# Even and odd time steps in rising order, output rows in transfers of up to 128 partitions, the filter folded in SBUF, and a new order of steps

## The chip, the cores and the metric

The kernel runs on one core of one Trainium2 chip. The metric is the device time of one execution in microseconds: three runs of the kernel before gave 217.42, 217.69 and 217.69, median 217.69 us. All durations come from one further, profiled execution.

## What is computed

Linear attention without softmax, an RMS norm per head, and then a gated long convolution over time. The sizes are 8 batches, 8 heads, 576 time steps, 64 channels a head, so 512 channels.

```python
kv = np.einsum('bhsd,bhse->bhde', k, v)
out = np.einsum('bhsd,bhde->bhse', q, kv)
rms = np.sqrt(np.mean(out * out, axis=-1, keepdims=True) + 1e-06)
x = out / rms * g_norm                      # heads side by side: [8, 576, 512]
x1, x2, x3 = split(x @ w_proj)              # three times 512 channels
x2_conv = irfft(rfft(x2, axis=1) * rfft(filter_fft, axis=0))
y = x1 * x2_conv * x3
return y @ w_out                            # float32 [8, 576, 512]
```

## The kernel before, in words

Nothing is looped. A table, ORDER, lists 725 steps in the form name.batch, and each step records its instructions in that order. Every engine (TensorE, VectorE, ScalarE, GpSimd, SyncE) works through its own queue strictly in the order in which the steps were recorded, and waits there for what the next instruction needs. A third number after a step's name puts so many matmuls of zeros (line 113) ahead of it on TensorE. PSUM is four pairs of banks; a step takes the pair that was given back first, and waits until it is free.

For one batch the steps are these.

- Loads. GpSimd's DMA queue brings k and v (128 partitions) and q (96 partitions, each with six successive time steps) and casts them to bf16. K is 72 matmuls for the heads' kv; eK copies them to SBUF. T (12 transposes on TensorE) or Qt (a transposing DMA on SyncE's queue) turns q; GpSimd's one-element copy Qh waits for such a transposing DMA.
- O: eight matmuls of 288 columns give two heads at a time, channels on the partitions and time along the free axis. sq (line 471) squares them on ScalarE, ob or ov (lines 478, 476) copy them times g_norm, R sums the squares over a head by a matmul, rs takes the inverse root, and x (line 503, VectorE) is the product. x holds the normalised input of one batch, 128 partitions by four head pairs by 576 steps.
- The gates. Ga and Gb are the projections to x1 and x3, 32 matmuls of 288 columns for each 128 channels and each of the two (line 645). x1 is copied by ScalarE (line 651), and g (line 653, VectorE) multiplies the other with it.
- The convolution. eo (line 515) adds and subtracts x and x backwards in time; fa and fr fold the three thirds of the sequence; rrM, rrT, abM, abT project the folded pieces with the middle part of w_proj; err, eab, eT copy the results to SBUF. F0, F1, F1t, F2, F2c are the transform over time as matmuls with tables of sines; M0 and M1 (line 620, VectorE) multiply with the filter's transform, M2 (line 635) does the third part; A0 and A1 (line 626) add the two halves of the products, mostly on GpSimd, as Av sometimes on VectorE. Io and I are the way back; vB, w and fin (lines 685 to 697, VectorE) recombine and multiply with the gates into yg. The step fin can be cut in two halves of time and two of channels (f001, f101, f023, f123; w likewise).
- The output. U (line 730) multiplies 256 rows of yg with w_out, U4 (line 743) 128 rows shared by two batches, ot copies to SBUF as float32, and SyncE's queue sends it. For the last batch single blocks of 128 rows (V, line 768) are copied by va or vv (line 774) and sent from SyncE's and GpSimd's queues (line 779).

Along the free axis time lies in 18 blocks of 32 steps: thirds of the sequence, and in each the residues of six. So 32 successive columns are 32 rows of the output six rows apart, and every 128-row block of output is sent in four transfers of 32 partitions each.

Ahead of the first batch a preamble builds the tables. Angles are made on VectorE, sines on ScalarE, Tb (TensorE) transposes them, and copies put them in SBUF. The filter is loaded (Lf) and folded by 36 matmuls of 512 columns with pieces of the identity and of a reversed identity (Ff, line 326). H0, H1, H2 (lines 343, 346) transform it; ScalarE scales one half of each result (lines 354, 357) and VectorE adds the other (line 359). 21 matmuls of zeros stand ahead of the first transposes.

Of the kernel before, what the change touches and what calls it, by code (L numbers as in the profile page):

```python
# [19 lines left out]
ORDER = """Z.0 Zi.0 Zd.0 Zr.0 Lqa.0 Zt.0 An2.0 An01.0 T0.0.21 Lf.0 eTv0.0 Zf.0 Tb0.0.4 Tb1.0 Tb2.0 Lqb.0 Lva.0 Ff0.0 Ff2.0.2  # L20
Ff1.0 Act.0 T1.0 Lka.0 Ka.0 eKa.0 eTv1.0 H1.0 Lkb.0 O01.0 Lvb.0 Kb.0.6 sq0.0 R0.0 sq1.0 eKab.0 rs0.0 O23.0.1 ov1.0
Lq.1 sq2.0 ov0.0 R1.0 R2.0.3 ov2.0 T0.1 Lw1.0 sq3.0 rs1.0 x0.0 Lv.1 Lw3.0 R3.0 Lk.1 rs2.0 ov3.0 eo0.0 eTv0.1 rs3.0
fr0.0 x1.0 H2.0 H0.0 eo1.0 HN1.0 Ga2.0 Ga1.0 Gb2.0 x12.0 Lw2.0 Gb1.0 Lqa.3 x11.0 T1.1 g2.0 K.1 eTv1.1 Ga0.0 g1.0 eK.1
x10.0 Lvb.2 fr1.0 O01.1 sq1.1 rrM.0 rrT.0 fa.0 HN0.0 sq0.1 abM.0 err.0 ov0.1 ov1.1 F0.0 abT.0 eab.0 Lk.2 Lqb.3 eT.0
O23.1 F2c.0 Lva.2 M0.0 F2.0 sq3.1 Lq.2 ob3.1 sq2.1 Qt.3 Gb0.0 ob2.1 M2.0 F1t.0 F1.0 R0.1 A0.0 R2.1 g0.0 rs0.1 Ga3.0
rs2.1 x13.0 R1.1 M1.0 K.2 rs1.1 Qt.2 R3.1 rs3.1 eK.2 Av1.0 Qh.3 Gb3.0 Io01.0 x.1 Io23.0 eo.1 I23.0 oa01.0 ea23.0
oa23.0 fr.1 Ga0.1 I01.0.1 ea01.0 g3.0 Ga1.1 fa.1 Lka.3 rrM.1 rrT.1 x10.1 Lva.3 x11.1 vB.0 Lkb.3 err.1 O01.2 sq1.2
abT.1 abM.1 sq0.2 w.0 Lvb.3 eT.1 ob1.2 Gb0.1 eab.1 f001.0 ob0.2 F0.1 f101.0 f023.0 Lwo.0 O23.2 g0.1 sq2.2 Ga2.1 ob2.2
Lva.4 M0.1 sq3.2 Gb1.1 ob3.2 x12.1 F2c.1 f123.0 F2.1 R1.2 R0.2 g1.1 F1t.1 F1.1 rs1.2 Lqb.4 M2.1 R2.2 K.3 rs0.2 rs2.2
Gb2.1 R3.2 eK.3 rs3.2 M1.1 Ga3.1 Lqa.4 g2.1 Lk.4 x1.2 A0.1 O23.3 x13.1 Av1.1 Lq.5 Gb3.1 sq2.3 sq3.3 x0.2 ob3.3 g3.1  # L30
U0.0 ob2.3 Ga2.2 Io01.1 ot0.0 x12.2 oa01.1 I23.1 Io23.1 I01.1 eo.2 oa23.1 fa.2 fr.2 abT.2 ea01.1 Lvb.4 R2.3 Ga3.2 eT.2
rs2.3 ev23.1 O01.3 sq0.3 abM.2 x13.2 sq1.3 vB.1 w.1 ob1.3 rrM.2 eab.2 rrT.2 K.4 F1t.2 ov0.3 F1.2 Qt.5 R0.3 err.2 eK.4
rs0.3 Gb3.2 R1.3 rs1.3 fin.1 M1.2 Gb2.2 R3.3 g3.2 A1.2 F0.2 U4.1 Qt.4 Lqa.7 g2.2 Ga0.2 rs3.3 Ga1.2 ot4.1 M0.2 x10.2
O23.4 F2c.2 x11.2 sq3.4 F2.2 U2.0 x.3 sq2.4 M2.2 ob3.4 Av0.2 ob2.4 eo.3 Gb1.2 I01.2 ot2.0 I23.2 ea01.2 g1.2 Gb0.2 Lv.5
Io01.2 ea23.2 g0.2 R2.4 rs2.4 oa01.2 Io23.2 U0.1 fa.3 ov23.2 O01.4 vB.2 abM.3 ot0.1 sq1.4 ob1.4 Lqa.6 fr.3 eab.3 abT.3
sq0.4 rrM.3 w.2 ob0.4 rrT.3 veT.3 Lk.5 f123.2 F2c.3 K.5 err.3 f001.2 f101.2 f023.2 F1t.3 F2.3 R3.4 eK.5 Lk.6 rs3.4
F1.3 U2.1 Ga0.3 M2.3 Lqb.7 ot2.1 M1.3 F0.3 x1.4 R0.4 R1.4 x10.3 Lv.6 rs1.4 rs0.4 Ga1.3 Gb1.3 x11.3 Lk.7 M0.3 A1.3 g1.3
O23.5 Gb0.3 sq3.5 g0.3 U0.2 A0.3 sq2.5 Lqb.6 ob2.5 ob3.5 I23.3 Ga2.3 x0.4 ea23.3 ov0r.2 Ga3.3 Qt.6 Io01.3 eo.4 fa.4
x13.3 Gb3.3 x12.3 fr0.4 Qh.6 fr1.4 oa01.3 Io23.3 oa23.3 I01.3 ea01.3 abT.4 g3.3 eT.4 vB.3 K.6 eK.6 O01.5 sq1.5 abM.4
sq0.5 ob1.5 eab.4 Gb2.3 w.3 g2.3 rrM.4 rrT.4 F1t.4 F1.4 ob0.5 R2.5 fin.3 Ga3.4 err.4 R1.5 rs2.5 x13.4 M1.4 Gb3.4 F0.4  # L40
A1.4 rs1.5 Lv.7 R0.5 Qt.7 g3.4 R3.5 rs0.5 rs3.5 U2.2 O23.6 M0.4 x.5 Qh.7 F2c.4 F2.4 U4.3 ot2.2 sq2.6 Ga2.4 ob2.6 ot4.3
sq3.6 eo.5 M2.4 ob3.6 U0.3 A0.4 Ga1.4 x12.4 ot0.3 I23.4 Io01.4 Gb2.4 xv1.4 I01.4 oa01.4 fa1.5 fr.5 Io23.4 ea23.4
oa23.4 g2.4 Gb1.4 O01.6 ev01.4 g1.4 sq0.6 rrM.5 rrT.5 R2.6 ob0.6 sq1.6 vB.4 fa0.5 ob1.6 w123.4 Ga0.4 Gb0.4 err.5 F0.5
xv0.4 abT.5 g0.4 rs2.6 R3.6 rs3.6 Ga3.5 x13.5 w101.4 w001.4 abM.5 veT.5 eab.5 Gb3.5 w023.4 M0.5 R0.6 K.7 fin.4 rs0.6
g3.5 F1t.5 F2c.5 A0.5 F2.5 F1.5 eK.7 R1.6 U2.3 rs1.6 M2.5 M1.5 ot2.3 x.6 Ga2.5 Gb2.5 O23.7 x12.5 sq3.7 sq2.7 A1.5 g2.5
U0.4 ob2.7 Ga1.5 ot0.4 Io23.5 ov3.7 eo0.6 eo1.6 I01.5 x11.5 oa23.5 Io01.5 fa.6 ea01.5 oa01.5 Gb1.5 g1.5 I23.5 R3.7
ea23.5 rs3.7 Ga0.5 fr.6 vB.5 x10.5 w101.5 w123.5 abM.6 abT.6 w023.5 eab.6 eT.6 O01.7 sq1.7 w001.5 Gb0.5 ob1.7 rrM.6
F2c.6 rrT.6 sq0.7 g0.5 F1t.6 fin.5 ob0.7 F2.6 err.6 F1.6 R0.7 M2.6 U0.5 F0.6 rs0.7 M1.6 ot0.5 Gb3.6 R1.7 rs1.7 Ga3.6
x13.6 Ga2.6 R2.7 M0.6 g3.6 Ga1.6 rs2.7 Gb2.6 x12.6 Av0.6 A1.6 x0.7 Io01.6 oa01.6 g2.6 x1.7 Ga0.6 x11.6 eo.7 Io23.6
fa.7 Gb1.6 I01.6 oa23.6 fr1.7 x10.6 ea01.6 fr0.7 I23.6 U2.5 abM.7 ea23.6 g1.6 vB23.6 eab.7 abT.7 rrM.7 vB01.6 w001.6  # L50
Gb0.6 veT.7 U4.5 F2c.7 g0.6 w123.6 rrT.7 ot2.5 F1t.7 err.7 w023.6 F1.7 f001.6 f023.6 f123.6 w101.6 Ga0.7 x10.7 M1.7
U2.4 ot2.4 F0.7 f101.6 F2.7 M0.7 ot4.5 Ga1.7 M2.7 A1.7 U0.6 x11.7 Gb0.7 g0.7 ot0.6 A0.7 Gb1.7 Io01.7 I01.7 g1.7 Io23.7
ev01.7 oa01.7 vB01.7 w101.7 Ga2.7 oa23.7 I23.7 Gb3.7 ea23.7 vB23.7 Ga3.7 U2.6 f101.7 x13.7 w023.7 Gb2.7 w001.7 w123.7
g3.7 f001.7 x12.7 g2.7 f123.7 ot2.6 V0a.7 V2a.7 V3.7 va3.7 V2b.7 va2.7 ds30.7 f023.7 V0b.7 vv0.7 dg31.7 U4.7 ds22.7
ds02.7 dg33.7 V1.7 dg21.7 dg00.7 dg01.7 dg03.7 dg23.7 va4.7 ds43.7 va1.7 dg32.7 dg10.7 dg20.7 ds40.7 ds41.7 ds11.7
ds12.7 ds42.7 dg13.7"""
# [3 lines left out]
def kernel(  # L60
# [128 lines left out]
    @one  # L189
    def Z(b):  # L190
        nc.scalar.preload_act_table_set("trig_and_small")
        vec.memset(nil, 0.0)
        vec.memset(ind, 0.0)
        for h in range(2):
            vec.memset(ind[64 * h:64 * h + 64, 64 * h:64 * h + 64], 1.0)  # L195
# [20 lines left out]
    def Zt(b):  # L216
# [7 lines left out]
        vec.tensor_scalar_mul(out=kturn, in0=kcol, scalar1=0.5 / S)
# [606 lines left out]
```

## Time and profile before

| | us |
|---|---|
| median of three runs | 217.69 |
| the profiled execution's own time | 218.32 |
| its span, first to last instruction | 216.6 |
| TensorE busy | 204.0 |
| VectorE busy | 183.6 |
| ScalarE busy | 146.4 |
| GpSimd busy | 68.2 |

The span is 1.7 us shorter than the profiled execution's own time, and that execution lies 0.6 us above the median. A busy time joins overlapping instructions: matmuls are pipelined, each is shown with its whole way through the array, and so a TensorE that is shown busy need not be at its peak rate.

### The profile page before, as it was taken

How to read it: one execution, taken by the hardware profiler on the slowest of the kernel's cores; microseconds unless marked ns; L12 is line 12 of the kernel's file. 1: busy time of each engine (PE TensorE's matmuls, PEld its weight loads, DVE VectorE, ACT ScalarE, POOL GpSimd, SP SyncE). 2: the span in 40 equal slices, each digit the busy share in tenths (PEclk: the TensorE clock that was granted, in tenths of full speed). 3: DMA queues.
4: the chain of work that ended last, by engine and by line, in shares of the span. 5: the costliest groups of instructions: out<-in, count | busy, mean ns of one | idle time of the engine just before them, and what ended most of it. 6: DMA issues, size and time to landing. Idle time of an engine off the chain costs nothing.

```text
span 216.6 us, 5016 instructions
## 1 busy us (share of the span) xinstructions
PE 204.0 (94%) x2043; PEld 120.4 (56%) x2043; DVE 183.6 (85%) x278; ACT 146.4 (68%) x235; POOL 68.2 (32%) x75
## 2 busy tenths in 40 slices
PE   7999999999999999998999996999999999999960
PEld 2444465476556656743676554665584685558620
DVE  7574896899999989998989897998989999897920
ACT  3659776777988995787669866566697554554440
POOL 8640304149070008501640083006500210044063
PEclk9999999999999999999999999999999999999996
DMA  4999999999999495999999719300330120426074
GB/s 53 202 205 206 209 205 207 205 191 172 207 205 195 115 136 103 201 239 247 210 199 183 137 10 241 100 3 3 97 97 3 26 70 3 98 50 193 7 204 133
DMA packets 37130, 30.16 MB, mean 139 GB/s; under 512 B 16194, under 2 KB 32578, under 8 KB 37106
## 3 DMA queue, kind: packets, MB, share of 16 engines
q0 software_dynamic: 17472, 17.57, 49.4%
q1 hardware_dynamic: 19634, 12.26, 25.3%
q8 instruction: 16, 0.26, 0.5%
q14 instruction: 8, 0.07, 0.1%
HBM read 33.69 MB, written 9.44 MB: 199 GB/s over the span
## 4 chain that ended last, share of the span: by engine, by line
PE 65%; issue 9%; DVE 7%; DMA 6%; POOL 6%; ACT 5%; POOLq 0%; ACTq 0%
PE ps L645 21%; PE ps L730 7%; DMA kb<-in_k_dram 6%; PE ps L113 5%; PE ps L557 4%; PE ps L675 3%; DVE tpw L620 3%; PE ps L543 3%; PE ps L468 2%; POOL out_dram L779 2%; PE ps L388 2%; POOL Y L626 2%; DVE eo L515 2%; PE ps L343 2%; PE ps L563 2%
## 5 line engine op out<-in xcount | busy, mean ns | idle before, releaser
L645 PE MATMUL ps<-x,wp 128*128 128x288 bf16 x512 | 71.3, 286 | 2.0 <-DVE Y L635 1.7
L645 PEld LDWEIGHTS <-wp 128*128 128x128 bf16 x512 | 48.9, 98 | 18.9 <-issue 3.6
L626 POOL TENSOR_TENSOR Y<-tpw 97x1024 bf16<-97x1024 f32 (+1 forms) x12 | 31.0, 2586 | 89.6 <-DVE tpw L620 89.6
L620 DVE TENSOR_TENSOR tpw<-ps,HH 97x2048 f32<-97x2048 f32 (+1 forms) x16 | 36.5, 2287 | 2.5 <-PE ps L601 1.3
L653 DVE TENSOR_TENSOR g<-ps,x 128x576 bf16<-128x576 f32 x32 | 24.1, 755 | 5.8 <-PE ps L645 3.3
L482 ACT ACTIVATE rstd<-ps 128x576 bf16<-128x576 f32 x32 | 20.4, 653 | 9.3 <-PE ps L468 9.0
L730 PE MATMUL ps<-wo,yg 128*128 128x512 bf16 x112 | 26.5, 379 | 0.0
L567 ACT CAST x<-ps 128x1024 bf16<-128x1024 f32 (+1 forms) x21 | 19.1, 917 | 9.6 <-PE ps L557 5.5
L679 ACT CAST ar<-ps 128x576 bf16<-128x576 f32 x28 | 17.1, 643 | 9.7 <-PE ps L676 9.6
L651 ACT CAST x<-ps 128x576 bf16<-128x576 f32 x30 | 18.9, 641 | 6.6 <-PE ps L645 6.2
L471 ACT ACTIVATE sq<-ps 128x576 bf16<-128x576 f32 x32 | 20.1, 655 | 2.7 <-PE ps L461 2.6
L734 ACT COPY ot<-ps 128x1024 f32<-128x1024 f32 x13 | 13.2, 1015 | 8.2 <-PE ps L730 8.1
L478 ACT ACTIVATE o<-ps,g_col 128x576 bf16<-128x576 f32 x24 | 17.8, 756 | 0.0
L730 PEld LDWEIGHTS <-yg 128*128 128x128 bf16 x112 | 10.7, 98 | 11.1 <-issue 0.5
L675 PE MATMUL ps<-IV,Y 128*128 128x192 bf16 x128 | 15.7, 245 | 0.0
L557 PE MATMUL ps<-wp,ab 128*128 128x512 bf16 x64 | 15.2, 380 | 0.0
L141 POOL DMA_DIRECT2D qb<-in_q_dram x13 | 9.6, 746 | 17.0 <-PE ps L468 10.8
L515 DVE TENSOR_TENSOR eo<-x 128x1152 bf16<-128x1152 bf16 (+1 forms) x20 | 14.5, 770 | 0.1
L113 PE MATMUL ps<-nil,ind 128*128 128x512 bf16 x38 | 12.3, 473 | 1.8 <-DVE ind L195 1.6
L676 PE MATMUL ps<-IV,Y 97*128 97x96 bf16 x64 | 13.2, 207 | 0.0
L468 PE MATMUL ps<-sq,ind 128*128 128x288 bf16 x64 | 12.5, 286 | 0.3 <-DVE HH L359 0.3
L697 DVE TENSOR_TENSOR yg<-w,g 128x576 bf16<-128x576 bf16 (+1 forms) x20 | 12.0, 632 | 0.1
(146 smaller groups left out, 312.7 us busy)
## 6 DMA issues: line engine op xcount, KB each, us to landing
out_dram<-ot SPq DMA_DIRECT2D x56, 128.0 KB, 2.3
kb<-in_k_dram POOLq DMA_DIRECT2D x6, 576.0 KB, 13.7
qb<-in_q_dram POOLq DMA_DIRECT2D x10, 288.0 KB, 8.5
vb<-in_v_dram POOLq DMA_DIRECT2D x8, 288.0 KB, 8.4
vb<-in_v_dram POOLq DMA_DIRECT2D x4, 576.0 KB, 12.5
qb<-in_q_dram POOLq DMA_DIRECT2D x3, 576.0 KB, 10.2
wp<-in_moe_w_proj_dram POOLq DMA_DIRECT2D x3, 512.0 KB, 17.4
kb<-in_k_dram POOLq DMA_DIRECT2D x4, 288.0 KB, 7.6
```

What stands on the lines that cost most here:

```text
L113: nc.tensor.matmul(pair[i][:, j], ind, nil, start=True, stop=True)
L471: act.activation(out=halves(sq()[:, j]), in_=tmp['o', b, j][:, :, 0:TH], func=AF.Square)
L482: act.activation(out=halves(rstd()[:, j]), in_=tmp['r', b, j][:, :, 0:TH], func=AF.Abs_reciprocal_sqrt, scale=1.0 / D, bias=1e-6)
L557: nc.tensor.matmul(pp[:, h], abt()[:, j, 2 * h * P:(2 * h + 1) * P], w2(j), start=(j == 0), stop=(j == NDC - 1))
L567: act.copy(out=o_(), in_=tmp[key, b])
L620: vec.tensor_mul(out=t_[:n], in0=xp[:n].unsqueeze(1).to_broadcast([n, 2, 2, DM]), in1=two)
L626: op(out=Yt()[:n, 2 * g:2 * g + 2], in0=t_[:n, ::-1, 0], in1=t_[:n, ::-1, 1])
L645: nc.tensor.matmul(pp[:, h, 0:TH], w_, x[:, j, h * TH:(h + 1) * TH], start=(j == 0), stop=(j == NDC - 1))
L651: ev0(out=x1, in_=pp[:, :, 0:TH])
L653: vec.tensor_mul(out=halves(g13t()[:, dc]), in0=pp[:, :, 0:TH], in1=x1)
L675: nc.tensor.matmul(pp[:, i, 0:SB], Y[:, 2 * g + h, cs], IV[:, 2 * g + h, 0:SB], start=(g == 1), stop=(g == 2))
L730: nc.tensor.matmul(pp[:, cc], ygt(b)[:, dc, b % 2 * 64 + c * P:b % 2 * 64 + (c + 1) * P], wo[:, dc], start=(dc == 0), stop=(dc == NDC - 1))
```

## The change

1. **Order of time.** The square and the copy of O (sq, ob, ov) write their 576 results a partition with a step of three elements, six bytes, so that the even time steps stand first in rising order and then the odd ones. Before they wrote in a row, and the matmul O read q in pieces of 32 columns; now it reads 288 in a row.
2. **Output.** 128 successive columns of yg are now 128 rows of the output two rows apart. The function send makes one transfer of 128 partitions, or of 256 rows in two blocks, where no border of even and odd lies inside, and cuts at the border otherwise (pieces of 96 and 32, or 64 and 64, partitions). U and U4 send the same way. The last batch sends U2 as one block of 256 rows and V0, V1 and U4 singly.
3. **The filter.** It is loaded as pairs of even and odd rows. Three matmuls with the reversed identity turn the odd rows round (Rv, line 344), copies bring them to SBUF (era, erv), and one addition and one subtraction on VectorE (ff0, ff1, line 352) fold it. The 36 matmuls of line 326 are gone. The transposes of the tables come in another cut (18 of 96 columns, 11 smaller ones), and the copies and the scaling of the H steps can go to either engine (hv on VectorE, ha on ScalarE): all three scalings go to VectorE.
4. **Order.** The table ORDER is written anew throughout. 19 matmuls of zeros stand ahead of the first transposes, and the memory that they read is cleared after the first steps of the angles instead of ahead of them.

The core of the diff:

```diff
-ORDER = """Z.0 Zi.0 Zd.0 Zr.0 Lqa.0 Zt.0 An2.0 An01.0 T0.0.21 Lf.0 eTv0.0 Zf.0 Tb0.0.4 Tb1.0 Tb2.0 Lqb.0 Lva.0 Ff0.0 Ff2.0.2
+ORDER = """Zj.0 Zi.0 Zf.0 Zk.0 Lqa.0 Z.0 Zm.0 Zt.0 Zd.0 Ad2.0 Zr.0 Lf.0 Zc.0 As2.0 Ad01.0 Zp.0 Ab2.0 Zh.0 T0.0.19 Ac2.0 Rv01.0.6
...
-        for odd in range(2):
-            for s in range(2):
-                for u in range(nb):
-                    nc.tensor.matmul(pp[32 * u:32 * u + 32, odd], w_, f[:, 5 - c if s else c], start=(s == 0), stop=(s == 1),
-                                     tile_position=(0, 32 * u))
+    def turn_mm(m0, m1):
+        pp = tmp['fr', m0] = take(("fr", m0), m1 - m0)
+        for m in range(m0, m1):
+            nc.tensor.matmul((pp[:, m - m0] if m1 - m0 > 1 else pp)[0:TR], rev, tmp['f'][:, 2 - m, 1], start=True, stop=True)
+    def fold(i, op):
+        op(out=folded[:, i], in0=tmp['f'][:, :, 0], in1=turned)
...
+    def h_scale(g, on_v):
+            if on_v:
+                vec.tensor_scalar_mul(out=o_, in0=i_, scalar1=s_)
+            else:
+                act.activation(out=o_, in_=i_, func=AF.Copy, scale=s_)
...
-                                 qT(b)[64 * r:64 * r + 64, 6 * j + 3 * hp:6 * j + 3 * hp + 3].rearrange("p c (m t) -> p m c t", m=3),
+                                 qT(b)[64 * r:64 * r + 64, 6 * j + 3 * hp:6 * j + 3 * hp + 3].rearrange("p c t -> p (c t)"),
...
+    def as_q(t):
+        return t.rearrange("p (a n c) -> p a c n", a=2, c=3)
-        act.activation(out=halves(sq()[:, j]), in_=tmp['o', b, j][:, :, 0:TH], func=AF.Square)
+        act.activation(out=as_q(sq()[:, j]), in_=o_ps(b, j), func=AF.Square)
...
+    def send(q, b, at, ot):
+        lots = [ot] if len(ot.shape) == 2 else [ot[:, 0], ot[:, 1]]
+        if len(lots) == 2 and at % TH + 2 * P <= TH:
+            q.dma_start(out=o_rows(b, at, [2 * P * DM, 2]), in_=ot)
+            return
+        for i, x in enumerate(lots):
+            a, p = at + i * P, 0
+            while p < P:
+                n = min(P - p, TH - (a + p) % TH)
+                q.dma_start(out=o_rows(b, a + p, n=n), in_=x[p:p + n])
+                p += n
-        for i in range(4):
-            nc.sync.dma_start(out=o_rows(b, 2 * (b % 2) + 4 * c0 + i, 2 * (b % 2) + 4 * c0 + 4 + i), in_=ot[32 * i:32 * i + 32])
+        send(nc.sync, b, b % 2 * 64 + c0 * P, ot)
```

Three places where instructions stand otherwise follow, as the built programs have them.

VectorE at batches 4 and 5, before: tpw is what M1 and M0 of batch 4 write, x the normalised input of batch 5, eo its folds, and the Y from ps and HM is M2 of batch 4.

```order
L620 TENSOR_TENSOR tpw<-ps_69,HH 128x2048
L653 TENSOR_TENSOR g_109<-ps_68,x_119 128x576
L620 TENSOR_TENSOR tpw<-ps_66,HH 97x2048
L503 TENSOR_TENSOR x<-o,rstd 128x2304
L515 TENSOR_TENSOR eo<-x 128x4x288 x2
L635 TENSOR_TENSOR Y<-ps_66,HM 128x1024
```

The same place now:

```order
L662 TENSOR_TENSOR tpw<-ps_66,HH 128x2048
L695 TENSOR_TENSOR g_111<-ps_68,x_116 128x576
L662 TENSOR_TENSOR tpw<-ps_69,HH 97x2048
L545 TENSOR_TENSOR x<-o,rstd 128x2304
L524 TENSOR_SCALAR o<-ps_69,g_col 128x2x3x96
L677 TENSOR_TENSOR Y<-ps_68,HM 128x1024
L557 TENSOR_TENSOR eo<-x 128x4x288 x2
```

Two instructions that read PSUM, a copy of O for batch 6 and M2, have moved between x and eo.

VectorE in the preamble, from the scaling of H1's result to the second half of x for batch 0, now (hu holds the scaled half of H1, H0 and H2 in turn, HH the filter's transform, o the copy of O):

```order
L387 TENSOR_SCALAR hu<-ps_66,cf 128x1024
L524 TENSOR_SCALAR o<-ps_67,g_col 128x2x3x96
L394 SCALAR_TENSOR_TENSOR HH<-ps_66,cf,hu 128x512 x2
L387 TENSOR_SCALAR hu<-ps_67,cf 97x1024
L394 SCALAR_TENSOR_TENSOR HH<-ps_67,cf,hu 97x512 x2
L545 TENSOR_TENSOR x<-o,rstd 128x1152
L387 TENSOR_SCALAR hu<-ps_66,pc 128x512 x2
L545 TENSOR_TENSOR x<-o,rstd 128x1152
```

Before, the last stretch of it, ahead of the second half of x for batch 0, was this (o is the copy of O, qT the turned q of batch 1):

```order
L503 TENSOR_TENSOR x<-o,rstd 128x1152
L476 TENSOR_SCALAR o<-ps_67,g_col 128x576
L515 TENSOR_TENSOR eo<-x 128x2x288 x2
L434 COPY qT<-ps_69 128x1152
L525 TENSOR_TENSOR x_475<-eo 128x384
L526 TENSOR_TENSOR rr<-x_475,eo 128x384
L503 TENSOR_TENSOR x<-o,rstd 128x1152
```

The work on the filter's transform has moved ahead of x, and the folds eo and fr of batch 0 behind it.

SyncE's queue at its end, before (ot, vb, kb and sq are the buffers from which the last rows are sent):

```order
L737 DMA out_dram<-ot 32x2x512 x8
L779 DMA out_dram<-vb_73 32x512
L779 DMA out_dram<-vb_72 32x512
L779 DMA out_dram<-kb_70 32x512
L779 DMA out_dram<-sq 32x512 x3
L779 DMA out_dram<-kb_71 32x512 x2
```

And now:

```order
L766 DMA out_dram<-ot 32x512
L766 DMA out_dram<-ot 96x512
L766 DMA out_dram<-ot 128x512
L760 DMA out_dram<-ot 128x2x512
L766 DMA out_dram<-kb_70 128x512
L766 DMA out_dram<-sq 64x512 x2
```

Of the last batch's own rows SyncE now sends four transfers, and GpSimd two (96 and 32 partitions) in place of eleven.

More of the change, by code (lines that the diff above doesn't have):

```diff
@@ L29 @@
[L29 to L33, printed above, removed]
@@ L39 @@
[L39 to L43, printed above, removed]
@@ new lines @@
+Tb1.0 Act.0 etv1.0 Tb0.0.4 etv0.0 ff0.0 eca1.0 ecv0.0 Lw1.0 Lk.1 Ka.0 eKaa.0 Kb.0.1 O01.0.2 eKb.0 sq1.0 ff1.0 H1.0
+R1.0.2 ob1.0 sq0.0 R0.0 hv1.0 rs1.0 T1.0.1 ov0.0 H0.0 rs0.0 eTa1.0 O23.0.1 hs1.0 H2.0.1 Lw3.0 Lv.1 hv0.0 sq2.0 sq3.0
+ob3.0 Lw2.0 R3.0 hs0.0 x0.0 hv2.0 rs3.0 R2.0 T1.1 rs2.0 ob2.0 x1.0 T0.1 eTa0.1 Lkb.2 Lq.2 hs2.0 Ga2.0.1 Ga3.0 Gb2.0
+eTa1.1 Hv1.0 Gb3.0 eo.0 fr.0 x13.0 x12.0 Lq.3 Lka.2 K.1 eK.1 g2.0 Ga1.0 O01.1 g3.0 HN0.0 sq0.1 rrM.0 Lv.2 x11.0 fa1.0
+rrT.0 sq1.1 ob1.1 fa0.0 ob0.1 verr.0 abM.0 eab.0 F0.0 abT.0.1 F2c.0 eT.0 O23.1 M0.0 F2.0 sq2.1 Gb1.0 ob2.1 sq3.1 F1t.0
@@ L336, in gen_h @@
[L336 removed]
+        hp = tmp['h', g] = take(("h", g))
         n = N1 if g == 0 else P
         for ri in range(2):
[L339 to L341 removed]
+            for m in range(3):
+                kw = dict(start=(m == 0), stop=(m == 2))
+                w_ = FH[0:TR, g, 2 * (0, 2, 1)[m] + ri]
                 if g < 2:
[L343 removed]
+                    nc.tensor.matmul(hp[:n, ri], w_[:, 0:n], folded[:, ri, m], **kw)
```

287 lines of the change are left out of this document (145 added, 142 removed).

## The prediction

> **What bounds the kernel now.** I read the page first, then a table of six stages, then who kept TensorE waiting.
>
> ```profile
> span 216.6 us, 5016 instructions
> PE 204.0 (94%) x2043; PEld 120.4 (56%) x2043; DVE 183.6 (85%) x278; ACT 146.4 (68%) x235; POOL 68.2 (32%) x75
> PE 65%; issue 9%; DVE 7%; DMA 6%; POOL 6%; ACT 5%; POOLq 0%; ACTq 0%
> ```
>
> TensorE is 94% busy and holds 65% of the chain that ended last. Busy means little with overlapping matmuls, so the stages (columns: stage, length, busy time and count of each engine, granted clock, DMA share, GB/s):
>
> ```profile
> 0.00:28.80 28.80, 26.62 (x255) 11.56 (x255) 19.89 (x68) 18.65 (x32) 12.71 (x25) 1.00 1.06 177
> 28.80:130.00 101.20, 99.68 (x1161) 60.68 (x1161) 93.17 (x111) 79.86 (x131) 34.40 (x34) 1.00 1.04 177
> 130.00:135.00 5.00, 3.33 (x22) 1.92 (x21) 4.14 (x3) 3.37 (x6) 1.72 (x1) 1.00 1.07 239
> 135.00:197.90 62.90, 62.90 (x538) 39.58 (x537) 57.71 (x80) 38.33 (x58) 13.97 (x5) 1.00 0.22 59
> 197.90:209.40 11.50, 11.42 (x76) 6.62 (x73) 8.68 (x19) 5.61 (x9) 1.70 (x4) 1.00 0.39 105
> 209.40:216.60 7.20, 0.00 (x0) 0.00 (x0) 0.00 (x0) 0.59 (x1) 3.75 (x8) 0.71 0.53 151
> ```
>
> From 28.8 to 209.4 TensorE works almost without a break, and VectorE is next with 93.17 of 101.20. Around it lie a preamble of 28.8 us and 7.2 us in which only the last rows go out. TensorE's waits, by line and by what ended them:
>
> ```profile
> PE ps L645 <- DVE Y L635: 1.7, 1, 1.7
> PE ps L113 <- DVE ind L195: 1.6, 1, 1.6
> PE ps L388 <- DMA kb<-in_k_dram: 0.9, 1, 0.9
> ```
>
> Between the stages there is little to win: 1.7 us once behind VectorE and 0.9 us once behind a load, with a few of 0.3 us or less. The matmuls of the eight batches are as many as before and as wide. So the change can win at three places, the preamble, these waits, and the end, and can lose in the middle wherever the new order makes TensorE wait.
>
> **The change, the preamble.**
>
> ```profile
> 1.62 7.65 PE ps L113 x21
> 14.16 1.83 PE ps L326 x20
> 28.86 4.03 PE ps L645 x32
> 35.83 0.97 PE ps L543 x4
> 1.60:7.20 5.60, 5.58 (x14) 2.00 (x15) 1.00 0.74 121
> 2.39 0.28 DVE L217 CAST kcol<-ki 128x1 f32<-128x1 int32 x1
> 3.60 0.29 DVE L224 TENSOR_SCALAR kturn<-kcol 128x3 f32<-128x3 f32 x1
> ```
>
> The first four rows are of the chain (start, length), the fifth a window over the zeros of line 113 alone, the last two of VectorE's timeline. The gates begin at 28.86, rrM of batch 0 at 35.83: that is my measure of the preamble.
>
> The zeros now wait for some 1.5 us of VectorE's work (lines 217 to 224, without the cast between them, and two memsets), so TensorE starts at about 3.3 instead of 1.62. Of the 21 zeros 14 started within 5.6 us, 0.43 us apart, though the record gives the clock as 1.00; the other seven took the rest of the 7.65, about 0.22 each. With 14 slow ones again, 19 end at 3.3 + 6.0 + 1.1 = 10.4; if eight are slow, at 9.2. I take 10.2, where before they ended at 9.27. Behind them come 12 transposes, six zeros and two reversing matmuls (0.5 + 1.3 + 0.45): the reversed filter stands in PSUM at 12.5. VectorE then has a chain of its own. Its prices:
>
> ```profile
> L328 DVE CAST yg<-ps 32x1024 bf16<-32x1024 f32 x1 | 1.2, 1212 | 0.9 <-PE ps L326 0.9
> L294 DVE COPY FW<-ps 128x768 bf16<-128x768 bf16 x1 | 0.5, 549 | 0.0
> L503 DVE TENSOR_TENSOR x<-o,rstd 128x1152 bf16<-128x1152 bf16 x8 | 6.0, 753 | 0.3 <-ACT rstd L482 0.3
> L686 DVE TENSOR_TENSOR bb<-ar 128x1536 bf16<-128x1536 bf16 x6 | 5.7, 952 | 0.0
> L359 DVE SCALAR_TENSOR_TENSOR HH<-ps,cf,hu 128x512 f32<-128x512 f32 x2 | 1.4, 746 | 2.0 <-ACT hu L354 2.0
> ```
>
> The copy of the reversed filter 1.2, a table 0.55, qT 0.75 and a table 0.55 bring it to 15.6; the last table is transposed on TensorE until about 16.2, so its copy ends at 16.7. The fold is two operations of 1536 (0.95 each) with 0.7 of small copies between: 19.2. H1 ends 0.8 later on TensorE, at 20.0. Then hv1 1.2, a copy of O 0.8, hs1 1.5, hv0 1.2, hs0 1.5, x 0.75, hv2 1.4 (two halves, priced as line 359) and the second x 0.75 make 9.1, less some 0.4 for the overlap of neighbours: 28.7. The first gate can do half its work ahead of that and ends at 29.2, where before it ended at 28.86 + 1.0 = 29.9 (32 matmuls in 4.03 us are four gates, 1.0 each). The 36 matmuls saved (the one row shows 20 of them in 1.83 us) are therefore not worth their own time: VectorE's three scalings and the late zeros take most of it back. Before rrM the transposes for batch 1 that stood behind the gates are now done (0.5), but rrM needs the bank that the third gate product frees, and ahead of it VectorE does hs2 1.5, a negation 0.4, eo 1.5, fr 1.1 and two products 1.5 from 28.7 on, less overlaps: 34.5. **Term one: 34.5 − 35.8 = −1.3**, between 0 (zeros slow throughout, the sines later than the tables want) and −2.4 (eight slow zeros, no wait on VectorE).
>
> [...]
>
> **The middle.** The wait of 1.7 us has its cause in this piece of the timeline:
>
> ```profile
> 128.03 1.35 DVE L503 TENSOR_TENSOR x<-o,rstd 128x2304 bf16<-128x2304 bf16 x1
> 129.38 2.34 POOL L626 TENSOR_TENSOR Y<-tpw 97x1024 bf16<-97x1024 f32 x1
> 129.41 3.60 DVE L515 TENSOR_TENSOR eo<-x 128x1152 bf16<-128x1152 bf16 x2
> 132.93 1.21 DVE L635 TENSOR_TENSOR Y<-ps,HM 128x1024 bf16<-128x1024 f32 x1
> ```
>
> GpSimd's addition starts the moment x ends, and the two eo take 3.60 us instead of twice 0.75 (the price of the same size in line 503). M2, line 635, comes 2.1 us late, and TensorE wants its bank. The new order has a copy of O and M2 between x and eo: together 0.8 + 1.2 = 2.0 us of work on PSUM, almost the whole of the 2.34 that GpSimd needs. The wait goes: −1.7. I looked through the other products that feed GpSimd's additions in the new order: nowhere else do two operations that read SBUF alone follow a product directly while an addition is due. [...]
>
> The load of k behind the 0.9 us stood on GpSimd's queue behind three others (half a q, v, half a q) that followed the addition for batch 2; now it is the first behind that addition, but output runs beside it: I take half of the wait, −0.4. Against these I set +0.4 for waits that I do not see. ScalarE gets five more copies of O that VectorE loses, the other moves nearly cancel, and both have the room in the table of stages.
>
> The strided writes of sq and ob are shown by no row. The nearest:
>
> ```profile
> L471 ACT ACTIVATE sq<-ps 128x576 bf16<-128x576 f32 x32 | 20.1, 655 | 2.7 <-PE ps L461 2.6
> L567 ACT CAST x<-ps 128x1024 bf16<-128x1024 f32 x16 | 16.3, 1018 | 8.8 <-PE ps L557 5.5 <-PE ps L550 2.9
> L567 ACT CAST x<-ps 128x512 bf16<-128x512 f32 x5 | 3.0, 591 | 0.7 <-PE ps L563 0.5
> L734 ACT COPY ot<-ps 128x1024 f32<-128x1024 f32 x13 | 13.2, 1015 | 8.2 <-PE ps L730 8.1
> ```
>
> An element costs (1018 − 591 of line 567's smaller form) / 512 = 0.83 ns whether two or four bytes are written, so the width of the write does not set it. I take nothing; the other end is a second step per element, 576 × 0.83 = 0.48 us for each of 61 instructions on ScalarE, a rival below. A gain is excluded: nothing less is written. **Term two: −1.7 − 0.4 + 0.4 = −1.7**, from −3.1 (all the waits named, and the small ones) to +2.3 (one such collision of 2.3 us elsewhere instead of here).
>
> **The end.** From 197.9, when Io and I of the first half of batch 7 are done, both kernels have the same TensorE work left, shown above as 76 matmuls in 11.50 us.
>
> ```profile
> L653 DVE TENSOR_TENSOR g<-ps,x 128x576 bf16<-128x576 f32 x32 | 24.1, 755 | 5.8 <-PE ps L645 3.3 <-PE ps L676 0.6 <-ACT ar L679 0.5
> L697 DVE TENSOR_TENSOR yg<-w,g 128x576 bf16<-128x576 bf16 x16 | 6.6, 451 | 0.0
> L774 ACT COPY vb<-ps 128x512 f32<-128x512 f32 x2 | 1.1, 588 | 2.0 <-PE ps L768 2.0
> 207.44 0.81 SPq L779 DMA_DIRECT2D out_dram<-vb  x2
> 212.65 0.50 POOL L779 DMA_DIRECT2D out_dram<-kb  x1
> out_dram<-ot SPq DMA_DIRECT2D x56, 128.0 KB, 2.3
> out_dram<-vb POOLq DMA_DIRECT2D x6, 64.0 KB, 2.3
> ```
>
> Before, the last block was in SBUF at 210.0, but 20 transfers of 0.4 to 0.5 us each stood in two queues, and the last was issued by 213.15; 2.3 us to land, and the span ended 3.45 us behind the issue. Now, counted from 197.9: the last gate ends at 4.8, its product (0.75), a half fin, and w and fin of the other pair (0.45 each) bring VectorE to 7.4. U of rows 320 to 576, which needs these halves, waits 0.9 us for them behind the U before it and ends at 9.1; the other halves end at 9.1 too; V0, V1 and U4 (12 matmuls, 2.6) end at 11.75. ScalarE copies ot (1.0), then three blocks of 0.59, the last until 12.75. Its two transfers are issued by 13.3, and 3.45 behind that is 16.75, where before 216.6 − 197.9 = 18.7. **Term three: −1.9**, from −2.5 to −0.9 (256 KB in flight per transfer instead of 64).
>
> **The sum.** −1.3 − 1.7 − 1.9 = −4.9: span 211.7, against the profiled execution's own 218.32 a time of 213.4, and against the median of the runs, 0.6 lower, 212.8. A measurement of this kernel tells about 0.2% from no change.
>
> **The rivals.**
> 1. *Everything falls early.* The zeros warm quickly (−1.1 more) and the middle has no new wait (−1.3 more): 210.4. For it: half the terms stand at cautious values. Against: VectorE at 92% of the middle leaves little slack. Chance 0.15.
> 2. *Only the end gains.* The preamble's VectorE chain runs into the sines and wins nothing (+1.3), and the waits move instead of going (+1.7): 215.8. For it: that chain is long and in strict order. Chance 0.14.
> 3. *VectorE's or a load's new waits eat all of it*, 4.9 us: within 0.2% of 217.7. Chance 0.04.
> 4. *Slower: ScalarE pays twice per element for the six-byte step.* Place: the chain O, sq, R, rs, x of every batch, where squares and copies stand one behind the other; eight of them add 3.8 us a batch and 29 us to 146.4 in all. For it: no row shows such a write, and ScalarE is in that chain of every batch. Against: 2.7 us is all that sq waited for O, but rs and the later copies waited on TensorE for longer, so the first 0.1 us or so an instruction is covered. It decides from about 0.25 us on, where a batch's 2 us exceed that; if 1.1 us of each batch's 3.8 reach TensorE, 8.8 us are added: 212.8 + 8.8 = 221.6. Chance 0.09.
>
> **How the numbers follow.** My forecast has 0.58: 212.8. Faster by over 0.2%: 0.58 + 0.15 + 0.14 = 0.87; the same 0.04; slower 0.09. The range takes in rivals 1 and 2 with a little beyond, 210.2 to 216.4; left out are rivals 3 and 4 and the fringes.
>
> **What would show it.** Right: rrM of batch 0 at about 34.5, reversed filter at 12.5, sq at 655 ns, no wait of TensorE behind line 677, and a last output transfer issued less than 2 us after TensorE's last matmul. Wrong: sq or ob above 0.9 us, gates of batch 0 not before 29, a long eo beside GpSimd's addition elsewhere, or a last transfer that takes longer to land than 3 us.

## The result, and the profile after

The changed kernel takes 233.37 us (median of four runs, 231.16 to 233.83); the kernel before, in the same session, 217.56. The ratio is 1.0709, 95% interval 1.0637 to 1.0781: slower by 7%, where 212.8 us was forecast. It is the fourth rival that came true, with about twice its price: the experiments below put the cost of the write with a step at 17.5 us, where 8.8 was set.

The page of the changed kernel, the rows that answer to those at the head of the prediction:

```profile
span 231.1 us, 4848 instructions
PE 203.3 (88%) x1996; PEld 122.0 (53%) x2018; DVE 183.4 (79%) x262; ACT 168.9 (73%) x239; POOL 58.0 (25%) x62
PE 57%; ACT 31%; issue 5%; DVE 4%; POOL 0%; POOLq 0%; DVEq 0%; ACTq 0%
```

VectorE and TensorE are as busy as before (183.4 and 203.3). ScalarE has 22.5 us more, and its share of the chain that ended last goes from 5% to 31%. Where the span became longer, the stages say, cut at the first gate of batch 0 (a gate is eight matmuls of 288 columns, so one batch has 32 for the four groups of 128 channels of x1 and 32 for x3), at the last 75 matmuls and at the last one's end (columns as in the prediction's table):

```profile
0.00:31.20 31.20, 23.75 (x239) 12.51 (x242) 21.89 (x62) 20.32 (x36) 12.68 (x25) 1.00 1.08 174
31.20:212.30 181.10, 168.17 (x1687) 102.92 (x1705) 153.97 (x184) 142.03 (x194) 44.29 (x36) 1.00 0.63 123
212.30:223.70 11.40, 11.34 (x75) 6.55 (x73) 7.52 (x18) 5.84 (x9) 0.00 (x0) 1.00 0.26 79
223.70:231.10 7.40, 0.01 (x1) 0.00 (x0) 0.00 (x0) 0.75 (x2) 1.06 (x2) 0.70 0.62 207
```

The preamble has 2.4 us more than before, the middle 12.0 (181.1 against 169.1), the last two stages together 0.1. In the middle TensorE now stands idle for 12.9 us (181.10 − 168.17); before it was 3.2. That is 9.7 of the 12.0; the other 2.3 are busy time (168.17 against 165.91, the granted clock at 1.00 in both), which was not followed up. Who kept it waiting, by line:

```profile
PE ps L511 <- ACT o L526: 3.6, 4, 1.3
PE ps L687 <- ACT o L526: 3.2, 6, 1.0
PE ps L112 <- DVE ind L195: 3.2, 1, 3.2
PE ps L511 <- ACT sq L520: 1.6, 2, 1.3
PE ps L585 <- ACT o L526: 1.0, 1, 1.0
```

Four of the five rows name the copy of O or its square, and with the smaller rows of this view those two come to 11.6 us (the 3.2 us of line 112 are the zeros' late start in the preamble). Both, in the groups by line:

```profile
L520 ACT ACTIVATE sq<-ps 128x576 bf16<-128x576 f32 x32 | 35.5, 1162 | 3.3 <-PE ps L504 3.1
L526 ACT ACTIVATE o<-ps,g_col 128x576 bf16<-128x576 f32 x29 | 34.1, 1214 | 0.0
L524 DVE TENSOR_SCALAR o<-ps,g_col 128x576 bf16<-128x576 f32 x3 | 3.6, 1191 | 2.2 <-ACT sq L520 2.2
```

The square takes 1.16 us where it took 0.655, at the same size; the copy 1.21 on ScalarE, where it took 0.756, and 1.19 on VectorE, where it took 0.812. The rows say nothing of the step of six bytes: the shapes in them are those of before. How this reaches TensorE is seen in a stretch of the timeline in batch 1 (start, length; in brackets the wait ahead and what ended it):

```profile
44.32 1.15 ACT L520 ACTIVATE sq<-ps 128x576 bf16<-128x576 f32 x1
...
44.83 1.14 PE L687 MATMUL ps<-x,wp 128*128 128x288 bf16 x8
...
45.26 1.20 ACT L526 ACTIVATE o<-ps,g_col 128x576 bf16<-128x576 f32 x1
...
46.25 1.18 ACT L520 ACTIVATE sq<-ps 128x576 bf16<-128x576 f32 x1
46.51 0.41 PE L637 MATMUL ps<-x,FT 64*64 64x512 bf16 x4 [0.54 <-ACT o L526]
...
47.22 1.21 ACT L526 ACTIVATE o<-ps,g_col 128x576 bf16<-128x576 f32 x1
```

Square and copy of two head pairs (a step O of eight matmuls makes two) are four instructions back to back, 4.1 us from 44.32 to 48.43. The pair of PSUM banks comes free only when the copy is done, here at 46.46, and TensorE's next step (line 637) needs it: it starts at 46.51, after a wait of 0.54.

### The profile page after: what moved, and what is told of

It reads as the page before. It is cut to its first block, busy times and chain, and to the rows that moved or that the text cites. A ratio compares the mean times of both kernels' runs of the same rounds, so it can differ in the third digit from the quotient of the medians.

```text
span 231.1 us, 4848 instructions
## 1 busy us (share of the span) xinstructions
PE 203.3 (88%) x1996; PEld 122.0 (53%) x2018; DVE 183.4 (79%) x262; ACT 168.9 (73%) x239; POOL 58.0 (25%) x62
## 4 chain that ended last, share of the span: by engine, by line
PE 57%; ACT 31%; issue 5%; DVE 4%; POOL 0%; POOLq 0%; DVEq 0%; ACTq 0%
PE ps L687 20%; ACT o L526 11%; ACT sq L520 10%; PE ps L785 8%; PE ps L112 5%; PE ps L716 4%; ACT x L609 4%; PE ps L511 3%; PE ps L599 2%; PE ps L432 2%; ACT kvblk L438 2%; PE ps L643 2%; ACT ot L789 1%; PE ps L585 1%; PE ps L629 1%
## 5 line engine op out<-in xcount | busy, mean ns | idle before, releaser
L668 POOL TENSOR_TENSOR Y<-tpw 128x1024 bf16<-128x1024 f32 (+1 forms) x11 | 28.0, 2552 | 87.4 <-DVE tpw L662 87.4
L520 ACT ACTIVATE sq<-ps 128x576 bf16<-128x576 f32 x32 | 35.5, 1162 | 3.3 <-PE ps L504 3.1
L526 ACT ACTIVATE o<-ps,g_col 128x576 bf16<-128x576 f32 x29 | 34.1, 1214 | 0.0
L785 PE MATMUL ps<-wo,yg 128*128 128x512 bf16 x114 | 28.0, 379 | 0.3
L693 ACT CAST x<-ps 128x576 bf16<-128x576 f32 x32 | 20.7, 651 | 9.0 <-PE ps L687 8.7
L789 ACT COPY ot<-ps 128x1024 f32<-128x1024 f32 x15 | 15.5, 1032 | 10.7 <-PE ps L785 10.7
L609 ACT CAST x<-ps 128x1024 bf16<-128x1024 f32 (+1 forms) x20 | 17.5, 893 | 6.4 <-PE ps L599 2.6
L785 PEld LDWEIGHTS <-yg 128*128 128x128 bf16 x120 | 11.5, 98 | 13.1 <-issue 1.0
L112 PE MATMUL ps<-nil,ind 128*128 128x512 bf16 x40 | 13.2, 453 | 3.9 <-DVE ind L195 3.2
L545 DVE TENSOR_TENSOR x<-o,rstd 128x2304 bf16<-128x2304 bf16 (+1 forms) x10 | 11.1, 1114 | 2.3 <-ACT o L526 1.7
L677 DVE TENSOR_TENSOR Y<-ps,HM 128x1024 bf16<-128x1024 f32 x8 | 9.8, 1223 | 3.3 <-PE ps L511 1.3
```

Source lines behind the costliest of these rows:

```text
L112: nc.tensor.matmul(pair[i][:, j], ind, nil, start=True, stop=True)
L520: act.activation(out=as_q(sq()[:, j]), in_=o_ps(b, j), func=AF.Square)
L526: act.activation(out=as_q(osb()[:, j]), in_=o_ps(b, j), func=AF.Copy, scale=g_col)
L609: act.copy(out=o_(), in_=tmp[key, b])
L668: op(out=Yt()[:n, 2 * g:2 * g + 2], in0=t_[:n, ::-1, 0], in1=t_[:n, ::-1, 1])
L693: ev0(out=x1, in_=pp[:, :, 0:TH])
```

## The experiments

Each run is compared with runs of the kernel before on its own chip; the ratios carry the comparison. "E3" below is the third run, which keeps the order of time with the step on the reading side.

### 1. Writes in a row

```diff
-        return t.rearrange("p (a n c) -> p a c n", a=2, c=3)
+        return t.rearrange("p (a n) -> p a n", a=2)
-        return tmp['o', b, j][:, :, 0:TH].rearrange("p a (c n) -> p a c n", c=3)
+        return tmp['o', b, j][:, :, 0:TH]
```

> The changed kernel with one thing undone: sq and the copy of O write their 576 results in a row again, so the time steps stand in the wrong order and the output rows are not the reference's. All else, the order of steps and the output transfers too, stays. Theory of the write: the step of six bytes costs every one of the 64 instructions about 0.5 us (sq 1.16 us instead of 0.655), and TensorE waits for them. Then sq is 0.65 to 0.67 us here, O's copy about 0.75, and the time falls to 214 to 218: the forecast of 212.8 and the 3 us by which the end after the last matmul was longer than forecast (8.2 us from it to the end of the span instead of 5.0). Theory of the order: the new order of steps itself makes TensorE wait, long writes or not. Then sq is short and the time stays above 225.

Measured: 214.41 us, ratio 0.9867 (0.9835 to 0.9898).

```profile
L526 ACT ACTIVATE o<-ps,g_col 128x576 bf16<-128x576 f32 x29 | 21.1, 750 | 0.0
L520 ACT ACTIVATE sq<-ps 128x576 bf16<-128x576 f32 x32 | 20.1, 654 | 3.4 <-PE ps L504 3.1
```

The step on the writing side is the whole slowdown, and more: without it everything else in the change makes the kernel faster by 1.3%. The theory of the order falls.

### 2. The step in TensorE's operand

```diff
-    qT(b)[64 * r:64 * r + 64, 6 * j + 3 * hp:6 * j + 3 * hp + 3].rearrange("p c t -> p (c t)"),
+    qT(b)[64 * r:64 * r + 64, 6 * j + 3 * hp:6 * j + 3 * hp + 3].rearrange("p c t -> p t c"),
```

with the writes in a row as in 1.

> The same computation as the changed kernel, with the step moved to the operand of the matmul O: it reads q's 288 columns in the order of time (three pieces of 96 in turn, a step of 192 bytes), and sq and the copy write in a row. Theory of the write: sq 0.65 to 0.67 us; if TensorE reads with a step at no cost, O's matmuls stay at 0.295 us each and the time is that of the run with writes in a row, within 0.5%; if it reads half as fast, 128 matmuls take up to 0.12 us more in pairs, some 8 us in all, and the time is 220 to 226. Theory of the order: above 225 in either case.

Measured: 219.36 us, ratio 1.0117 (1.0060 to 1.0174).

```profile
L504 PE MATMUL ps<-qT,kvblk 64*64 64x288 bf16 x128 | 12.4, 456 | 0.3 <-ACT kvblk L438 0.2
```

The square is 0.653 again, but the matmul O, 0.295 in run 1, takes 0.456: TensorE pays for a step in the operand that streams. The time lies just below the 220 to 226 that were set for a reading at half speed. Against run 1 it costs 2.5%, less than the step in the write, and more than the change brings.

### 3. The step in the reading of PSUM (E3)

```diff
-        return t.rearrange("p (a n c) -> p a c n", a=2, c=3)
+        return t.rearrange("p (a n c) -> p a n c", a=2, c=3)
-        return tmp['o', b, j][:, :, 0:TH].rearrange("p a (c n) -> p a c n", c=3)
+        return tmp['o', b, j][:, :, 0:TH].rearrange("p a (c n) -> p a n c", c=3)
```

The two loops over c and n change places on both sides: the write runs in a row, the read jumps 384 bytes.

> The same computation as the changed kernel, with the step moved to the reading side of sq and of the copy: they read PSUM with a step of 384 bytes, three at a time, and write SBUF in a row. Theory of the write (only a write of two bytes with a step costs): sq 0.65 to 0.67 us, and the time is that of the run with writes in a row, within 0.5%. Theory that a step costs on either side, or that many short rows in the access pattern cost: sq is 1.1 us or more, and the time stays at 231 to 235 or above.

Measured: 215.31 us, ratio 0.9903 (0.9866 to 0.9940). The stages, cut as above:

```profile
0.00:28.60 28.60, 23.67 (x239) 12.45 (x242) 21.48 (x62) 17.24 (x36) 12.26 (x24) 1.00 1.06 169
28.60:194.70 166.10, 163.75 (x1686) 101.81 (x1704) 153.29 (x184) 122.21 (x194) 44.65 (x36) 1.00 0.72 137
194.70:206.20 11.50, 11.41 (x76) 6.60 (x74) 7.58 (x18) 5.88 (x9) 0.00 (x0) 1.00 0.30 97
206.20:212.50 6.30, 0.00 (x0) 0.00 (x0) 0.00 (x0) 0.71 (x2) 1.06 (x2) 0.77 0.64 215
```

The square takes 0.654, the copy 0.750 on ScalarE and 0.815 on VectorE: reading PSUM with a step is free here (in run 1 the square takes 0.654 and the copy 0.750). Its waits name the copy of O nowhere. This kernel does all that the changed one does and is faster than it and than the kernel before; from here on it is the base. From the changed kernel's span of 231.1 its span differs by 18.6 us: 2.6 in the preamble, 15.0 in the middle, 1.0 at the end. By the ratios, which rest on all runs, it is 17.5 us: the profiled execution of E3 was the fastest of its four (214.34, median 215.31).

### 4. The step alone, in the kernel before

The diff of run 1 the other way round, in the kernel before.

> The kernel before, with one part of the change alone: sq and the copy of O write with the step of six bytes; order of steps, filter and output transfers are the old ones, and the output rows are not in the reference's order. Theory of the write: sq 1.16 us, O's copies about 1.2, ScalarE busy 146 + 28 = 174 us, and the time 228 to 240, more than the changed kernel's or near it, since the old order was not laid out for long copies either. Theory of the order: the old order hides them, and the time is 221 at most.

Measured: 233.28 us, ratio 1.0747 (1.0692 to 1.0803), the squares 1.161 us, ScalarE 167.4 us busy. They cost 7.5% in the old order and 8.1% in the new one (1.0709 against 0.9903): the old order does not hide them either. Busy came out lower than the 174 expected, for the most part because neighbours on ScalarE overlap more with the step: by some 0.22 us in the changed kernel, where in the kernel before it is 0.12.

### 5 and 6. Half the dose

sq alone with the step, then the copy alone; the other in a row.

> Half the dose: sq alone writes with the step of six bytes, the copy of O writes in a row. 32 instructions are 0.51 us longer, 16.2 us of ScalarE's time in place of 32. If every long write reaches TensorE in the same share (18.6 of 32 us with all of them), the time is 215.3 + 9.4 = 224.7. If the waits that ScalarE has anyway cover the first part, as the forecast's fourth rival had it (0.25 us an instruction, half of the full dose, covered), it is 218 at most.

> The other half: the copy of O alone writes with the step, sq in a row. 29 instructions on ScalarE are 0.46 us longer and three on VectorE 0.38, 14.5 us in all. By an equal share 215.3 + 8.4 = 223.7; if the first part is covered, 218 at most. If the copy is the one that stands in TensorE's way (the matmuls for the sum wait for it on ScalarE's queue, x comes later) and the square is not, this run is at 225 and the other near 217.

Measured: 221.57 us, ratio 1.0197 (1.0171 to 1.0223), for sq; 220.33 us, ratio 1.0148 (1.0116 to 1.0180), for the copy. Against E3's 0.9903 that is 2.9% and 2.5%, 6.4 and 5.3 us. Together they cost 8.1%, 17.5 us. None of the three expectations holds as it stands: the two apart make 11.7 us and both together 17.5, half as much again, so the cost rises faster than the dose. A part is covered: of 16.2 us of longer squares 6.4 reach the time, of 14.5 us of longer copies 5.3, of both together (30.7) 17.5. But neither half is covered whole, as rival 4 would have it, and neither of the two alone is the one that matters.

### 7. The price by itself

Behind E3's last step 26 groups of three copies each; in ScalarE's first five (lines 869 to 873) and in line 874 this is what is written, then pairs, their partner in a row, and float32:

```python
    for _ in range(3): act.copy(out=st(D16, 1), in_=P2)   # 869; steps 2, 3, 4, 8 in 870 to 873
    for _ in range(3): act.copy(out=s3(D16), in_=P3)      # 874: the pattern of the change
    # 875: pairs, 4 bytes together, 12 bytes apart; 876: the same 288 elements in a row
    # 877 to 879: float32, steps 1, 2, 3; 880: PSUM read with a step of three
```

> The disputed cost by itself: the kernel that reads PSUM with the step, and behind its last step 26 groups of three copies of 576 elements a partition into a scratch buffer (one group of pairs and one beside it have 288), so its own time says nothing. ScalarE, bf16 from PSUM, written with a step of 1, 2, 3, 4 and 8 elements; the pattern of the changed kernel; pairs (4 bytes together, 12 bytes apart); float32 with steps of 1, 2, 3; PSUM read with a step of three; bf16 from SBUF with steps of 1 and 3. VectorE and GpSimd likewise, fewer. Theory of the two-byte write: every bf16 write with a step of 2 or more elements takes 1.1 us, whatever the step, pairs and float32 with a step cost nothing (0.6 us, 0.4 for 288), VectorE the same. Theory of the distance: the price grows with the step in bytes, float32 with a step of 3 pays too. Theory of the number of rows in the pattern: only the pattern of the changed kernel and the pairs pay.

```profile
L873 ACT CAST yg<-ps 128x576 bf16<-128x576 f32 x3 | 8.1, 2702 | 0.1
L872 ACT CAST yg<-ps 128x576 bf16<-128x576 f32 x3 | 4.3, 1431 | 0.1
L871 ACT CAST yg<-ps 128x576 bf16<-128x576 f32 x3 | 3.3, 1113 | 0.1
L874 ACT CAST yg<-ps 128x576 bf16<-128x576 f32 x3 | 3.3, 1112 | 0.1
L879 ACT COPY yg<-ps 128x576 f32<-128x576 f32 x3 | 2.7, 915 | 0.1
L870 ACT CAST yg<-ps 128x576 bf16<-128x576 f32 x3 | 2.4, 797 | 0.1
L878 ACT COPY yg<-ps 128x576 f32<-128x576 f32 x3 | 2.0, 663 | 0.1
L869 ACT CAST yg<-ps 128x576 bf16<-128x576 f32 x3 | 1.9, 649 | 0.1
L880 ACT CAST yg<-ps 128x576 bf16<-128x576 f32 x3 | 1.9, 638 | 0.1
L875 ACT CAST yg<-ps 128x288 bf16<-128x288 f32 x3 | 1.2, 403 | 0.1
L876 ACT CAST yg<-ps 128x288 bf16<-128x288 f32 x3 | 1.2, 398 | 0.1
```

For bf16 out of PSUM the time grows with the step: 0.65, 0.80, 1.11, 1.43 and 2.70 us for steps of 1, 2, 3, 4 and 8 elements, from 2 on by 0.32 us for each element of step, or 0.55 ns per element written. That the price grows with the step is the theory of the distance; that of the two-byte write, whatever the step, falls, and so does that of the number of rows (line 874 is as long as the plain step of three in 871). The distance in bytes is not all of it, though. At a step of 8 bytes float32 takes 0.663 us and bf16 1.431. Float32 with 12 bytes from one element to the next takes 0.92 where a row takes 0.64, but pairs of bf16, written together and 12 bytes apart too, cost nothing (403 against 398 ns). What in the write makes the price, these rows don't say. VectorE out of PSUM pays the same, 0.757, 0.797 and 1.114 us for steps of 1, 2 and 3. PSUM as the source is not needed for it: from SBUF a step of three takes ScalarE from 0.671 to 1.146, VectorE from 0.310 (0.492 at two) to 0.647, and GpSimd from 0.663 to 1.142. All this is one execution with three instructions a group, alike within 4 ns but for line 869 (638 to 672).

### 8. The output transfers undone

In send every transfer is cut into pieces of 32 partitions, in E3.

> The kernel that reads PSUM with the step and writes in a row, with the output transfers undone: each is sent in pieces of 32 partitions again, from the same queues. Theory that the number of issues sets the end (the forecast's third term): behind TensorE's last matmul SyncE has twelve transfers of 0.43 us in place of four, its last issue comes 1.5 to 2 us later, and the time rises from 215.3 to 216.8 to 217.3. Theory that the end is set by the 1.28 MB that are still to be moved in those 6 us, however they are cut: 215.3 within 0.5 us.

Measured: 217.75 us, ratio 1.0021 (0.9999 to 1.0043), 1.2% or 2.6 us above E3. SyncE's last issues, E3 and then this run:

```profile
204.95 0.39 SPq L760 DMA_DIRECT2D out_dram<-ot  x1
206.45 0.34 SPq L766 DMA_DIRECT2D out_dram<-kb  x1
206.94 1.62 SPq L766 DMA_DIRECT2D out_dram<-sq  x2
```

```profile
207.55 2.31 SPq L761 DMA_DIRECT2D out_dram<-ot  x4
210.03 1.76 SPq L767 DMA_DIRECT2D out_dram<-kb  x4
211.88 1.78 SPq L767 DMA_DIRECT2D out_dram<-sq  x4
```

With pieces the last issue ends 5.1 us later (213.66 against 208.56), though the last matmul ends only 0.2 later. That is more than the 1.5 to 2 us expected, since SyncE's queue is late already when the last rows come: its transfers of the block before end at 207.45, in E3 at 204.85. The span is 3.7 longer, since the last small piece is through 1.4 us sooner behind its issue. The number of issues sets this end, as the third term had it.

### 9. eo in its old place

```diff
-sq2.6 ov3.6 M2.4 U0.3 eo.5 Ga0.4
+sq2.6 eo.5 ov3.6 M2.4 U0.3 Ga0.4
```

> The same kernel with one step moved back: eo of batch 5 stands right behind x again, ahead of the copy of O and of M2 of batch 4, as in the kernel before. [...] Theory that the wait moves along and was never worth its own length: eo is long, and the time stays at 215.3 within 0.4 us.

Measured: 218.76 us, ratio 1.0079 (1.0055 to 1.0103), 1.8% or 3.8 us above E3, more than twice the wait of 1.67 us that the kernel before had at this place. The timeline of the place, and below it the granted clock (the column behind the engines) in windows of 2 us:

```profile
126.83 3.29 POOL L668 TENSOR_TENSOR Y<-tpw 97x1024 bf16<-97x1024 f32 x1
...
127.94 3.46 DVE L557 TENSOR_TENSOR eo<-x 128x1152 bf16<-128x1152 bf16 x2
...
131.33 0.81 DVE L524 TENSOR_SCALAR o<-ps,g_col 128x576 bf16<-128x576 f32 x1
132.05 1.21 DVE L677 TENSOR_TENSOR Y<-ps,HM 128x1024 bf16<-128x1024 f32 x1
132.19 1.14 PE L687 MATMUL ps<-x,wp 128*128 128x288 bf16 x8 [2.52 <-DVE o L524]
```

The same two instructions in E3:

```profile
127.40 3.29 POOL L668 TENSOR_TENSOR Y<-tpw 97x1024 bf16<-97x1024 f32 x1
130.48 1.49 DVE L557 TENSOR_TENSOR eo<-x 128x1152 bf16<-128x1152 bf16 x2
```

And the clock in run 9:

```profile
132.00:134.00 2.00, 1.81 (x14) 1.41 (x14) 1.97 (x4) 0.64 (x1) 0.00 (x0) 0.80 1.08 373
134.00:136.00 2.00, 2.00 (x17) 1.80 (x15) 1.29 (x3) 0.73 (x2) 0.00 (x0) 0.50 1.17 267
136.00:138.00 2.00, 2.00 (x18) 1.54 (x17) 0.88 (x3) 0.81 (x2) 0.00 (x0) 0.85 1.24 255
```

eo takes 3.46 beside GpSimd's addition, where in E3 it starts as the addition ends and takes 1.49. Everything behind it is late, the copy of O too, which the kernel before did not have at this place. TensorE waits 2.52 us, and then the clock falls to 0.5. It is full again from 138 on, and in the three windows (0.20 + 0.50 + 0.15) × 2 = 1.7 us of work is lost, which makes 4.2 in all. The span is 3.4 longer than E3's; most of the rest is that this execution had a preamble 0.6 us shorter (rrM of batch 0 at 34.6).

### 10. The last 256 rows in two blocks

```diff
-U2.7 w023.7 ot2.7
+V2.7 V3.7 w023.7 va2.7 dg2.7 va3.7 ds3.7
```

> The kernel that reads PSUM with the step, and at the end the last 256 rows are two single blocks, copied and sent one by one from GpSimd's and SyncE's queues, in place of one block of 256 rows from SyncE's. Theory that the bytes set the end: the first 256 KB leave half a us earlier, and the time falls by 0.3 to 0.6 us from 215.3. Theory that latency and issues set it: no change or 0.3 us more.

Measured: 214.63 us, ratio 0.9876 (0.9842 to 0.9910). The interval overlaps E3's (0.9866 to 0.9940), and the span behind the last matmul is 6.5 us where E3 has 6.3, so no gain is shown. Whether it is better than E3 its runs don't settle.

## Why the prediction was wrong, point by point

**The step that failed** is this one, in the second term: "0.83 ns whether two or four bytes are written, so the width of the write does not set it. I take nothing". Both rows compared there wrote in a row. That four bytes cost what two do says nothing of a hop between elements, and no row shown there had a hop. The other end stood right behind it, 0.48 us for each of the instructions; runs 1, 3 and 7 show 0.51 for the square and 0.46 for the copy. In place of nothing, 61 instructions on ScalarE and three on VectorE became 0.4 to 0.5 us longer each, and 17.5 us of that reached the time. The sign that the prediction had named for being wrong, sq or ob above 0.9 us, came with 1.16 and 1.21. The bound was there and was kept out of the second term's range, which ended at +2.3.

**Rival 4** had the place (the chain O, sq, R, rs, x) and, at this step, the price of one instruction. That price was met by luck: its reason was that ScalarE pays twice per element, 2 × 0.83 ns, and run 7 shows a price that grows with the step (0.15 us more than a row at two elements, 0.46 at three, 0.78 at four, 2.05 at eight), which passes twice the element's price only near three. Its price in all, 8.8 us, rested on 1.1 of 3.8 us reaching TensorE in a batch. The runs show 17.5 us in all, 2.2 a batch, and from half the dose, 16 or 14 us of longer instructions, already 6.4 or 5.3. A point from which it decides, with everything below it covered, was not found. The timeline of batch 1 shows one place of the kind: the copy holds the banks that TensorE wants next, so there a longer square or copy reaches it at once. A chance of 0.09 was too little for a cost that no row bounded and that sits on 61 instructions of one engine.

**The rest of the sum** can be read from E3, which has all of the change but the step of the write: 212.5 us of span, where 211.7 was forecast. That looks nearer than it is. The profiled execution of the kernel before lay 0.6 us above its median (218.32 against 217.69), that of E3 1.0 below its own. By the runs E3 gains 2.1 us (1.3 to 2.9), less than half of the 4.9 forecast. The terms below are differences between one execution of each, 4.1 us in all; which of them is the smaller in a usual execution is not shown. E3's chain, in the preamble:

```profile
5.67 11.52 DMA kb<-in_k_dram
17.23 0.48 PE ps L432 x36
35.21 0.38 PE ps L585
```

- *The preamble*, −1.3: −0.6 (35.2 at rrM of batch 0; 34.5 forecast, 35.8 before). The six executions of the new order with short writes that were profiled have 34.3 to 35.3, so the number forecast lies within what one execution differs from the next. Its path was another, and in so far it is luck: the sum went along VectorE's chain of tables and scalings. What ends last is a load of k, for which the second half of K waits; from there the chain runs over the filter's transform on TensorE and ScalarE's squares, copies and roots to the gates. In run 1 that load let TensorE go 1.15 us earlier, at 16.08, and the gates began 0.84 earlier, at 27.72 against 28.56: a view of the loads belonged into the forecast. The late zeros, which ended at 9.9, do not appear in that chain. For eight slow ones, the far end of this term, 9.2 was worked out; the zeros end at 9.25 in run 1 and at 9.89 in the changed kernel and E3, and what sets the number of slow ones no run shows. Loads in another order were not tried.
- *The middle*, −1.7: −2.6 (194.7 − 35.2 = 159.5, before 197.9 − 35.8 = 162.1). The wait of 1.7 us is gone as forecast: in E3 eo takes 1.49 at the same place, from the end of GpSimd's addition on, and run 9, where it takes 3.46 beside the addition, brings the wait back (2.52). The copy of O and M2, which now stand between x and eo, keep their lengths in E3 (0.815 and 1.221 by line; before 0.812 and 1.220). Why eo grows longer beside the addition no run shows. The wait of 0.9 us for k is gone from the middle altogether, and of the 0.4 set aside for waits unseen nothing came: −1.7 − 0.9 = −2.6.
- *The end*, −1.9: −0.9 (17.8 us from the cut at 194.7 instead of 18.7). TensorE's share is 11.5 as in the kernel before, where 11.75 was forecast. Behind the last matmul it is 6.3, not 5.0: two pieces of 64 partitions took SyncE 1.62 us where 0.55 was taken, so that the last issue ends 2.4 us behind the matmul instead of 1.55, and the span ends 3.9 behind that issue, not 3.45.

Together −4.1 of −4.9 in these two executions, −2.1 by the runs: two of the three terms were taken too large, one too small, and that the sum of the spans comes out near is luck. The changed kernel itself has rrM of batch 0 at 37.6 and a middle of 174.7 us; from E3 it differs only in the side of the square and of the copy that carries the step.

## What to carry to other kernels

When an access pattern changes on one side of an instruction, look for a row that has such a pattern on that side, and where there is none, put the instruction at its far end with a fair chance, times its count. A permutation between PSUM and SBUF can be put on the read of PSUM or on the write to SBUF by exchanging two loops, and here the read was free (the square 0.654 us) and the write cost 0.5 us in 576 elements (1.16). Where the write must jump, pairs of bf16, 12 bytes apart, cost nothing here (run 7, 403 against 398 ns for 288 elements). A stall can cost more than its length: in run 9 a wait of 2.52 us was followed by a granted clock of 0.80, 0.50 and 0.85 in three windows of 2 us, 4.2 us in all. And compare forecasts with the runs, not with one profiled execution: here the two differ by 2 us.
